# An attention and two-MoE kernel: value splitting and row scaling taken off GpSimd beside the attention, two fills and two weight splits put at its ends

## The chip, the cores and the metric

One core of a Trainium2 chip runs the whole program. The metric is the device time of one execution in microseconds (us), taken as the median of several executions. The engines are called TensorE (PE in the rows, PEld for its weight loads), VectorE (DVE), ScalarE (ACT), GpSimd (POOL) and SyncE (SP, which here only issues transfers).

## The reference

Three stages, each feeding the next, all in float32:

```python
scores = scale * q @ k.T                      # B, H, S, D = 2, 8, 768, 64
keep = is_sink | in_window                    # 4 sink columns, window 128
a = softmax(where(keep, scores, -1e9)) ; x = a @ v       # -> [1536, 512]
...
logits = x @ w_gate + modality_bias[modality_id]         # 8 experts
e_idx = argmax(logits) ; gate_w = probs[e_idx]
out[mask] = gate_w * (relu(x[mask] @ w1[e]) @ w2[e])     # routed MoE, F = 1024
...
P = exp(x @ w_gate2 - max) ; 8 x { rows /= sum ; columns /= sum ; P *= N/E }
out += P[:, e] * (relu(x @ w1[e]) @ w2[e])               # dense MoE, 8 experts
```

## The kernel before, in words

**Attention (`attention_fast`, L161-532).** There are 8 groups (batch b, pair of heads g) of 6 tiles of 128 query rows: 48 units. A unit is a chain over four engines. TensorE multiplies queries and keys (`sc`, L351), VectorE adds the mask and takes the row maximum (`pt`, `bias`, L353), ScalarE takes the exponential (L355), TensorE transposes (`tq`, L363), ScalarE and VectorE split the result into a high and a low 16-bit part (`ph` L381, `pl` L391), and TensorE multiplies both with the values (`po`, L409-L412). VectorE scales the result into `x_b` (L420-L425). Beside this, the four sink columns go through a small product: `psk` (L371 on ScalarE for its high part, L375 on VectorE for its low part), `tk` (L386) and L403. The loop (L477-529) handles a different phase of three neighbouring units in each turn.

**Values.** A group's values `raw_v` are prepared while the group ahead of it runs (`prep`, lists `e`, `m0`, ... at L329 ff. say in which turn). The scale is `vinv` (`r.inv`). For the first group ScalarE writes the high part with the scale (L327) and VectorE the low part (L328). For the other seven groups GpSimd multiplies `raw_v` in place (`v_sc`, L276, 128x768), ScalarE copies the high part (`v_hi`, L273, twice) and GpSimd subtracts (`v_lo`, L279, twice). GpSimd also makes the sink rows of the values (L289-L294).

**Routing of batch 0** runs as generator steps (`Steps`) inside the loop once its rows are there (from unit 18 on): logits, arg-max and positions on VectorE (`route`, L784-971). Then `scatters` (L749) multiplies each of 6 row tiles by its gate on GpSimd (L753) and writes its rows to their places in DRAM with an indirect transfer from GpSimd (L754). `weights0` (L772) loads the first expert's weights in quarters (q = 0, 1; tile `r`) and splits each into a high part on ScalarE (L780) and a low part (L781), for q = 0 on GpSimd and for q = 1 on VectorE. Its first split starts at turn `SPLIT0` = 43 ("late"), the others follow one turn at a time.

**Routed MoE (`routed`, L1290).** It multiplies the scattered rows (`xrow`, transposed at L986 and split into `xh`, `xl` at L991, L997) with the split weights (L1135, L1145); later weight quarters are split at L731. **Dense MoE** (L1509-1595) does the same for 8 experts with seven products in place of eight per block (`bk` L1518, `y` L1572).

**What sets the order.** The order on ScalarE and GpSimd in the attention is that of the program text (`manual_schedule`, L475); on VectorE and TensorE a scheduler orders the instructions after the first units. Each engine works through its own list in order. The start (`setup_consts`, L54) ends with `fi` (L105), which all engines load (L106) before they branch into `attention_fast` (L1086); behind the branch VectorE builds the masks (`masks_a`, L192) and GpSimd clears `xrow` (L662).

## Time and profile before

| | |
|---|---|
| median of 3 runs | 1295.49 us (1295.07 to 1298.07) |
| the profiled execution | 1297.28 us, span 1295.3 us |
| mean granted TensorE clock | 0.986 of full speed |
| busy share of the span: TensorE, VectorE, ScalarE, GpSimd | 97%, 74%, 45%, 34% |
| attention up to the first routed product | 0 to 149.33 us |
| dense MoE, TensorE alternating between L1518 and L1572 | about the last 870 us |

The span is the time from the first to the last instruction; the profiled execution adds what lies around it. A busy TensorE is not TensorE at its peak, since its matmuls overlap and their ends are modelled. The attention is 12% of the span, and its engines' loads differ from stage to stage, so the page's shares over the whole span say little of it; it has to be read by windows.

### The profile page before, as it was taken

Reading aid. Unit: us, or ns where it says so; the run is one execution under the profiler, and the core shown is the slowest. Engines: PE = TensorE matmul, PEld = TensorE weight load, DVE = VectorE, ACT = ScalarE, POOL = GpSimd, SP = SyncE. Lnnn points to the kernel's source line nnn. Section 1 sums busy time; section 2 is a strip of 40 time slices with the busy share of each in tenths; the row PEclk is TensorE's granted clock in tenths of the full one; section 3 lists DMA queues with packets and bytes.
Section 4 is the critical chain, followed back from the end, with each engine's and each line's share of the span. In section 5 each row is a group of like instructions: output and inputs, shape, how many; then the busy total and the mean of one; then the engine's idle time right before and its main releaser. Section 6 shows DMA issues by size and latency. Waiting matters only on the chain.

```text
span 1295.3 us, 19403 instructions
## 1 busy us (share of the span) xinstructions
PE 1250.8 (97%) x7201; PEld 748.4 (58%) x7201; DVE 958.5 (74%) x2096; ACT 582.2 (45%) x1087; POOL 446.1 (34%) x434
## 2 busy tenths in 40 slices
PE   6999799999899999999999999999999999999997
PEld 4666589998554555555555555555555555555553
DVE  7978585448599777777777777777777777777764
ACT  5876524556444364343433344343433344343431
POOL 2436230338503333333333334333333333333323
PEclk9998899999899999999999999999999999999999
DMA  6433626632101112121111112121111112221002
GB/s 132 109 68 122 186 82 198 195 110 72 50 5 37 37 39 54 40 53 38 37 37 38 37 37 49 46 54 37 37 38 37 37 38 46 48 53 38 5 1 97
DMA packets 114300, 80.16 MB, mean 62 GB/s; under 512 B 50196, under 2 KB 97300, under 8 KB 114196
## 3 DMA queue, kind: packets, MB, share of 16 engines
q1 hardware_dynamic: 112276, 72.51, 22.5%
q0 software_dynamic: 1920, 6.32, 1.3%
q8 instruction: 59, 0.97, 0.3%
q14 instruction: 45, 0.37, 0.1%
HBM read 71.94 MB, written 6.87 MB: 61 GB/s over the span
## 4 chain that ended last, share of the span: by engine, by line
PE 66%; DVE 3%; issue 3%; POOL 1%; ACT 1%; POOLq 0%; DVEq 0%
PE y L1572 35%; PE bk L1518 31%; DVE cb L1530 1%; DVE hl L1527 1%; POOL out_dram L1592 0%; DVE x L1585 0%; ACT hh L1524 0%; DVE xlo L1225 0%; ACT x L1583 0%; DVE wmax L1025 0%; DVE scr__6108 L1500 0%; POOL w2l L1082 0%; DVE pp L1501 0%; DVE pp L1493 0%; DVE xmm L1020 0%
## 5 line engine op out<-in xcount | busy, mean ns | idle before, releaser
L1585 DVE SCALAR_TENSOR_TENSOR x<-y,pps,x 128x512 f32<-128x512 f32 x332 | 243.8, 747 | 115.8 <-PE y L1572 115.7
L1572 PE MATMUL y<-w2h,hh 128*128 128x512 f16 x768 | 291.8, 380 | 1.0 <-DVE x L1585 0.5
L1572 PE MATMUL y<-w2l,hh 128*128 128x512 f16 x768 | 291.7, 380 | 0.0
L1572 PE MATMUL y<-w2h,hl 128*128 128x512 f16 x768 | 291.6, 380 | 0.0
L1530 DVE SCALAR_TENSOR_TENSOR cb<-bk,cb 128x384 f32<-128x384 f32 x384 | 189.8, 549 | 84.3 <-PE bk L1518 84.3
L1572 PEld LDWEIGHTS <-hh 128*128 128x128 f16 x1536 | 150.7, 98 | 174.9 <-issue 2.2
L1518 PEld LDWEIGHTS <-w1h 128*128 128x128 f16 x1792 | 175.4, 98 | 125.4 <-issue 4.6
L1059 POOL TENSOR_TENSOR xrow<-raw2a 128x256 f32<-128x256 f32 x160 | 112.6, 738 | 292.4 <-issue 245.0
L1524 ACT ACTIVATE hh<-cb 128x384 f16<-128x384 f32 x256 | 126.4, 523 | 174.5 <-DVE cb L1530 174.5
L1532 ACT ACTIVATE cb<-bk 128x384 f32<-128x384 f32 x64 | 31.3, 489 | 302.2 <-PE bk L1518 298.2
L1076 POOL TENSOR_TENSOR w1l<-raw2a,w1h 128x256 f16<-128x256 f32 x64 | 51.3, 821 | 300.3 <-ACT w1h L1064 300.3
L1518 PE MATMUL bk<-x_b,w1h 128*128 128x384 f16 x448 | 146.8, 328 | 1.7 <-DVEq L1423 1.7
L1518 PE MATMUL bk<-x_b,w1l 128*128 128x384 f16 x448 | 146.8, 328 | 0.0
L1518 PE MATMUL bk<-xl,w1h 128*128 128x384 f16 x448 | 146.8, 328 | 0.0
L1518 PE MATMUL bk<-xhi,w1l 128*128 128x384 f16 x448 | 146.0, 326 | 0.0
L1518 PE MATMUL bk<-xlo,w1h 128*128 128x384 f16 x448 | 146.0, 326 | 0.0
L1518 PE MATMUL bk<-xhi,w1h 128*128 128x384 f16 x448 | 146.0, 326 | 0.0
L1527 DVE SCALAR_TENSOR_TENSOR hl<-cb,hh 128x384 f16<-128x384 f32 x256 | 132.2, 557 | 8.0
L1572 PEld LDWEIGHTS <-hl 128*128 128x128 f16 x768 | 75.3, 98 | 91.1 <-issue 0.8
L1518 PEld LDWEIGHTS <-w1l 128*128 128x128 f16 x896 | 87.9, 98 | 58.4 <-issue 0.7
L1077 POOL TENSOR_TENSOR w1l<-xrow,w1h 128x1280 f16<-128x1280 f32 x32 | 84.7, 2647 | 0.1
L1082 POOL TENSOR_TENSOR w2l<-raw2b,w2h 128x1024 f16<-128x1024 f32 x32 | 68.7, 2148 | 12.6 <-ACT w2h L1081 12.6
(370 smaller groups left out, 1884.1 us busy)
## 6 DMA issues: line engine op xcount, KB each, us to landing
raw2b<-in_moe_w_dram SPq DMA_DIRECT2D x40, 512.0 KB, 3.8
raw2a<-in_moe_w_dram SPq DMA_DIRECT2D x64, 256.0 KB, 3.0
r<-in_moe_w_dram SPq DMA_DIRECT2D x24, 512.0 KB, 6.5
raw2a<-in_moe_w_dram SPq DMA_DIRECT2D x8, 512.0 KB, 5.0
wall<-dmax SPq DMA_DIRECT2D x32, 128.0 KB, 4.0
xrow<-scr SPq DMA_DIRECT2D x4, 832.0 KB
raw_v<-in_v_dram SPq DMA_DIRECT2D x8, 384.0 KB, 4.0
raw_k<-in_k_dram SPq DMA_DIRECT2D x14, 192.0 KB, 2.8
```

Source lines behind the costliest of these rows:

```text
L1059: nc.gpsimd.tensor_tensor(ws[:, s_], x, y, op)
L1076: nc.gpsimd.tensor_tensor(wl[:, 4 + i], w1_block(n, i, i), wh[:, 4 + i], ALU.subtract)
L1077: nc.gpsimd.tensor_tensor(wl[:, 0:5], ws, wh[:, 0:5], ALU.subtract)
L1082: nc.gpsimd.tensor_tensor(vl, raw2[n % 2][1], vh, ALU.subtract)
L1518: nc.tensor.matmul(bank, w[wi][:, WSLOT[m], k], X[xi][sb][m - 1][:, k], start=(first and i == 0), stop=(i == 5), skip_group_check=True)
L1524: nc.scalar.activation(h[0][:, i, l], cb[:, 2 * i + l], AF.Relu)
L1527: nc.vector.scalar_tensor_tensor(h[1][:, i, l], cb[:, 2 * i + l], 0.0, h[0][:, i, l], ALU.max, ALU.subtract)
L1530: nc.vector.scalar_tensor_tensor(x[0], bank, sign * HSC, x[1], ALU.mult, ALU.add)
L1532: nc.scalar.activation(c22, b0, AF.Copy, scale=HSC)
L1572: nc.tensor.matmul(y, h[hi_][:, i, l, t * P:(t + 1) * P], w[wi][:, i], start=(i == 0 and pi == 0), stop=(i == 1 and pi == 2))
L1585: nc.vector.scalar_tensor_tensor(dst, y, f if e == 0 else pps[n % 3][:, T:T + 1], acc, ALU.mult, ALU.add)
```

## The change

Five edits. **(1)** `v_sc` (L276) goes; for every group ScalarE writes the high part with the scale and VectorE makes the low part from `raw_v`, the scale and the high part in one instruction. **(2)** The first two mask instructions and the window's difference `wp` move from behind the branch to ahead of it. **(3)** `xrow` is cleared before the branch. **(4)** The row scaling of batch 0 (6 instructions) moves from GpSimd to ScalarE; that of batch 1, in the routed stage, stays. **(5)** The four splits of the first weights run at the ends of the loop's last four turns (46 to 49) in the order w1 of q 0, w1 of q 1, w2 of q 0, w2 of q 1, all low parts on GpSimd; each is followed by its own load of the next quarter.

```diff
-def setup_consts(nc, c, cp, a, first):
+def setup_consts(nc, c, cp, xp, a, first):
...
     nc.vector.tensor_copy(fi, fl[0:1, 3:4])
+    c.mk = xp.tile([P, 3, P + SB], F32, name="mk")
+    c.mtmp = xp.tile([P, P], F32, name="mtmp")
+    c.wp = xp.tile([P, 1], F32, name="wp")
+    keep_window(nc, c, c.mk[:, 2, SB:], c.dcur, c.mtmp)
+    nc.vector.tensor_single_scalar(c.wp, c.win, -float(P), ALU.add)
     c.fast = nc.values_load(fi[0:1, 0:1], engines=mybir.ALL_ENGINES, min_val=0, max_val=1)
...
     def masks_a():
-        nc.vector.tensor_single_scalar(tmp, c.dcur, 0.0, ALU.is_ge)
-        nc.vector.scalar_tensor_tensor(cur, c.dcur, c.win, tmp, ALU.is_lt, ALU.mult)
...
-        nc.vector.tensor_single_scalar(w1, c.win, -float(P), ALU.add)
-        nc.vector.tensor_scalar(prev, c.dcur, w1, None, ALU.is_lt)
+        nc.vector.tensor_scalar(prev, c.dcur, c.wp, None, ALU.is_lt)
...
         def v_hi(h):
-            nc.scalar.activation(r.vs[:, h, :, 0:DH], d["v"][:, h], AF.Copy)
-
-        def v_sc():
-            nc.gpsimd.tensor_tensor(rv, rv, r.inv.unsqueeze(2).broadcast_to([P, G * NT, DH]), ALU.mult)
+            nc.scalar.activation(r.vs[:, h, :, 0:DH], d["v"][:, h], AF.Copy, scale=r.inv)
 
         def v_lo(h):
-            nc.gpsimd.tensor_tensor(r.vs[:, h, :, V1:], d["v"][:, h], r.vs[:, h, :, 0:DH], ALU.subtract)
+            nc.vector.scalar_tensor_tensor(r.vs[:, h, :, V1:], d["v"][:, h], r.inv, r.vs[:, h, :, 0:DH], ALU.mult, ALU.subtract)
...
-        m0 = [[], [], [vs1], [], [vinv, v_sc], [], [], []]
+        m0 = [[], [], [vs1], [], [vinv], [], [], []]
...
-        if i == SPLIT0:
-            ready.append("late")
...
         steps.run("pool")
+        if i >= len(units) - 2:
+            steps.run("w")
...
-        setup_consts(nc, c, cp, a, first)
+        setup_consts(nc, c, cp, xp, a, first)
+    nc.gpsimd.memset(xrow, 0.0)
...
-        nc.gpsimd.memset(xrow, 0.0)
...
     def scatters(b, bank):
         xb = x_bs[b]
         for t in range(NT):
-            yield "pool", 2 if t else 0
-            nc.gpsimd.tensor_tensor(xb[:, t, 0:D], xb[:, t, 0:D], gs[:, t:t + 1].broadcast_to([P, D]), ALU.mult)
+            yield "pool" if b else "act", 2 if t else 0
+            if b:
+                nc.gpsimd.tensor_tensor(xb[:, t, 0:D], xb[:, t, 0:D], gs[:, t:t + 1].broadcast_to([P, D]), ALU.mult)
+            else:
+                nc.scalar.activation(xb[:, t, 0:D], xb[:, t, 0:D], AF.Copy, scale=gs[:, t:t + 1])
+                yield "pool", 0
...
-        for q in range(2):
-            for i in range(2):
-                yield ("act", 1) if q or i else ("late", 0)
+        for i in range(2):
+            for q in range(2):
+                yield "w", 0
                 h, l = wqs[q][2 * i:2 * i + 2]
                 nc.scalar.activation(h, raws[q][i], AF.Copy)
-                (nc.vector if q else nc.gpsimd).tensor_tensor(l, raws[q][i], f32(h), ALU.subtract)
-            load_raw(q, *wsrc(ex), 2 + q)
+                nc.gpsimd.tensor_tensor(l, raws[q][i], f32(h), ALU.subtract)
+                load_part(q, i, *wsrc(ex), 2 + q)
```

The lines of the changed kernel lie some 5 lower from L276 on, so that L353 is L348 there, L391 is L386, L375 is L370, and L780 and L781 are L785 and L786.

**VectorE around the branch.** First the list before, from `fi` on (`TENSOR_LOAD` and the comparison are the branch):

```order
L105 CAST fi<-fl 1x1
L106 TENSOR_LOAD fi
L1086 COMPARE_AND_BRANCH
L195 TENSOR_SCALAR mtmp<-dcur 128x128
L896 MEMSET tf 128x1
L196 SCALAR_TENSOR_TENSOR mk<-dcur,val,mtmp 128x128
L197 SCALAR_TENSOR_TENSOR mk<-jrow,val,mk 128x128
```

and the same place now:

```order
L104 CAST fi<-fl 1x1
L114 TENSOR_SCALAR mtmp<-dcur 128x128
L115 SCALAR_TENSOR_TENSOR mk<-dcur,val,mtmp 128x128
L109 TENSOR_SCALAR wp<-val 128x1
L110 TENSOR_LOAD fi
L1091 COMPARE_AND_BRANCH
L197 SCALAR_TENSOR_TENSOR mk<-jrow,val,mk 128x128
```

The window mask (`mtmp`, `mk`) and `wp` now stand between `fi` and VectorE's own load of it.

**VectorE in group 0, where the values of group 1 are split**, before (the two ISA rows of L353 are one masking step):

```order
L425 TENSOR_TENSOR x_b_76<-po,rc 128x2x128
L353 ISA pt,bias<-sc,mk 128x260
L353 ISA bias 128x1
L391 SCALAR_TENSOR_TENSOR pl<-tq,ph 128x512
L353 ISA pt,bias<-sc,mk 128x260
L353 ISA bias 128x1
L353 ISA pt,bias<-sc,mk 128x260
L353 ISA bias 128x1
L665 CAST mf<-mi 128x12
L420 TENSOR_SCALAR rc<-po,vinv 128x4
```

and now, where L274 is the low part of the values and L348 the masking step:

```order
L420 TENSOR_TENSOR x_b_76<-po,rc 128x2x128
L348 ISA pt,bias<-sc,mk 128x260
L348 ISA bias 128x1
L386 SCALAR_TENSOR_TENSOR pl<-tq,ph 128x512
L274 SCALAR_TENSOR_TENSOR vs<-raw_v,vinv,vs 128x6x64
L348 ISA pt,bias<-sc,mk 128x260
L348 ISA bias 128x1
L660 CAST mf<-mi 128x12
L348 ISA pt,bias<-sc,mk 128x260
L348 ISA bias 128x1
```

One low part now stands right behind a unit's `pl`, ahead of the next masking step; the second (not shown) stands behind the `pl` after it in the same way.

**ScalarE at the end of the attention**, before (`w1h`, `w2h` are the weights' high parts, L991 the high part of the routed rows):

```order
L780 ACTIVATE w2h_226<-r_1_219 128x1024
L371 ACTIVATE psk<-pt 128x16
L381 ACTIVATE ph<-tq 128x512
L388 ACTIVATE skT<-tk 24x128
L381 ACTIVATE ph<-tq 128x512
L388 ACTIVATE skT<-tk 24x128
L991 ACTIVATE xh<-tp 128x4x104 x4
```

and now:

```order
L376 ACTIVATE ph<-tq 128x512
L383 ACTIVATE skT<-tk 24x128
L785 ACTIVATE w1h_227<-r_0_223 128x1024
L376 ACTIVATE ph<-tq 128x512
L383 ACTIVATE skT<-tk 24x128
L785 ACTIVATE w1h_231<-r_1_225 128x1024
L785 ACTIVATE w2h_229<-r_0_224 128x1024
L996 ACTIVATE xh<-tp 128x4x104
L785 ACTIVATE w2h_233<-r_1_226 128x1024
L996 ACTIVATE xh<-tp 128x4x104 x3
```

Three of the four high parts now stand behind the last unit's `ph` (row L376), two of them ahead of the first L996 (L991 before) and one ahead of the other three. GpSimd's list ends with the four low parts in the same order and nothing between them, and on SyncE's list each is followed by the load that overwrites its raw quarter.

## Rows read from the trace of the kernel before

**Rows 1.** Windows behind the attention: us; busy (count) of PE, PEld, DVE, ACT, POOL; PEclk, DMA.

```profile
149.33:156.00 6.67, 6.67 (x26) 6.08 (x27) 0.00 (x0) 1.78 (x3) 0.00 (x0) 0.56 1.05 279
...
338.00:1295.30 957.30, 942.81 (x5029) 492.07 (x5029) 721.36 (x1401) 386.62 (x664) 312.05 (x285) 0.99 0.17 39
```

**Rows 2.** The same view, the attention: 17 units, then four times 6, then 5.

```profile
21.55:59.75 38.20, 37.85 (x388) 26.29 (x387) 35.86 (x149) 32.96 (x94) 14.06 (x26) 1.00 0.45 98
59.75:77.54 17.79, 17.32 (x160) 11.15 (x159) 12.05 (x50) 13.62 (x38) 5.51 (x11) 1.00 0.30 68
77.54:94.39 16.85, 16.45 (x178) 11.56 (x176) 14.74 (x68) 13.66 (x39) 5.26 (x10) 1.00 0.29 63
94.39:113.46 19.07, 17.31 (x133) 11.62 (x132) 17.75 (x75) 11.96 (x34) 11.51 (x16) 0.75 0.65 194
113.46:128.88 15.42, 14.35 (x144) 10.13 (x141) 13.33 (x52) 11.60 (x34) 11.07 (x16) 0.97 0.14 53
128.88:142.95 14.07, 9.59 (x85) 6.17 (x83) 12.71 (x32) 11.15 (x26) 6.79 (x9) 0.88 0.66 174
```

**Rows 3.** Line 375 alone: its durations, then its VectorE time (count) in those windows.

```profile
L375 DVE SCALAR_TENSOR_TENSOR psk<-pt,psk x32: 124/161/3405, 21.1 to 142.2; 128x8 f16<-128x8 f32 x32
...
21.55:59.75 38.20, 5.05 (x11) 1.00 0.45 98
94.39:113.46 19.07, 3.05 (x4) 0.75 0.65 194
113.46:128.88 15.42, 3.61 (x4) 0.97 0.14 53
128.88:142.95 14.07, 4.01 (x4) 0.88 0.66 174
```

**Rows 4.** Timeline behind the branch: start, duration, engine, line, instruction, [idle before <-releaser].

```profile
7.37 2.04 DVE L195 TENSOR_SCALAR mtmp<-dcur 128x128 f32<-128x128 f32 x1 [0.77 <-DVE fi L105]
7.44 1.81 POOL L662 MEMSET xrow<- 128x2048 f32 x1
```

**Rows 5.** Timeline at the first scatters.

```profile
98.85 1.17 POOL L754 DMA_INDIRECT scr<-x_b,pos  x1 [0.29 <-POOL x_b L753]
...
99.32 1.81 DVE L375 SCALAR_TENSOR_TENSOR psk<-pt,psk 128x8 f16<-128x8 f32 x1
...
100.05 1.05 POOL L753 TENSOR_TENSOR x_b<-x_b,rs 128x512 f32<-128x512 f32 x1
```

**Rows 6.** Timeline at the first weights' parts.

```profile
132.03 2.34 POOL L781 TENSOR_TENSOR w1l<-r,w1h 128x1024 fp32r<-128x1024 f32 x1
...
133.31 3.40 DVE L375 SCALAR_TENSOR_TENSOR psk<-pt,psk 128x8 f16<-128x8 f32 x1
...
136.77 0.23 PE L386 MATMUL tk<-ident_h,psk 128*24 128x128 f16 x1 [3.27 <-DVE psk L375]
```

**Rows 7.** Groups by line, up to 150 us: count | busy, mean ns | idle before.

```profile
L780 ACT ACTIVATE w1h<-r 128x1024 fp32r<-128x1024 f32 x2 | 2.1, 1040 | 0.0
L796 ACT ACTIVATE xT<-tp 128x512 f32<-128x512 f32 x6 | 3.5, 582 | 2.6 <-PE tp L792 2.6
L327 ACT ACTIVATE vs<-raw_v,vinv 128x384 f16<-128x384 f32 x2 | 1.1, 608 | 0.0
L328 DVE SCALAR_TENSOR_TENSOR vs<-raw_v,vinv,vs 128x384 f16<-128x384 f32 x2 | 1.1, 616 | 0.0
```

**Rows 8.** Line 279: idle of GpSimd before it and what ended it; us, times.

```profile
  ACT vs L273: 18.1, 13
```

**Rows 9.** Timeline from the attention's end into the routed stage.

```profile
145.55 0.55 PE L986 MATMUL tp<-ident,xrow 104*128 104x104 f32 x4 [0.48 <-DVE rc L422]
...
149.33 0.72 PE L1135 MATMUL pt<-xh,w1h 128*128 128x416 f32 x1 [3.23 <-issue]
...
160.08 1.05 ACT L731 ACTIVATE w1h<-r 128x1024 fp32r<-128x1024 f32 x1
```

**Rows 10.** Transfers: KB each, us from issue to landing.

```profile
r<-in_moe_w_dram SPq DMA_DIRECT2D x24, 512.0 KB, 6.5
```

More of the change, by code (lines that the diff above doesn't have):

```diff
@@ L41 @@
 LOAD_LAG = 6
-SPLIT0 = 43
 GW = P // KC
@@ L183, in attention_fast @@
     R = 3 * G * NS
-    mk = cp.tile([P, 3, P + SB], F32, name="mk")
-    tmp = cp.tile([P, P], F32, name="mtmp")
-    w1 = cp.tile([P, 1], F32, name="w1")
+    mk = c.mk
     hm = cp.tile([R, 3, G], F32, name="hm")
@@ L227, in prep @@
         bnk = {}
-        rv = d["v"].rearrange("p h t d -> p (h t) d")
         vd = r.vs.rearrange("p h t w -> p (h t) w")
@@ L326, in v_c @@
                 for h in range(G):
-                    nc.scalar.activation(r.vs[:, h, :, 0:DH], d["v"][:, h], AF.Copy, scale=r.inv)
-                    nc.vector.scalar_tensor_tensor(r.vs[:, h, :, V1:], d["v"][:, h], r.inv, r.vs[:, h, :, 0:DH], ALU.mult, ALU.subtract)
+                    v_hi(h)
+                    v_lo(h)
             r.v_s = v_sink
@@ L721, in body, with load_part @@
     wqs = [new_wq(wr, i) for i in range(2)]
+    def load_part(i, j, w1, w2, q):
+        if j:
+            nc.sync.dma_start(raws[i][1], w2.rearrange("o (k p) f -> p (o k) f", p=P)[:, q * FC:(q + 1) * FC, :])
+        else:
+            nc.sync.dma_start(raws[i][0], w1.rearrange("o (k p) f -> p (o k) f", p=P)[:, :, q * FQ:(q + 1) * FQ])
     def load_raw(i, w1, w2, q):
-        nc.sync.dma_start(raws[i][0], w1.rearrange("o (k p) f -> p (o k) f", p=P)[:, :, q * FQ:(q + 1) * FQ])
-        nc.sync.dma_start(raws[i][1], w2.rearrange("o (k p) f -> p (o k) f", p=P)[:, q * FC:(q + 1) * FC, :])
+        for j in range(2):
+            load_part(i, j, w1, w2, q)
     def split_w(ri, wi, pool_lo=False):
@@ L751, in scatters @@
         for t in range(NT):
-            yield "pool", 2 if t else 0
-            nc.gpsimd.tensor_tensor(xb[:, t, 0:D], xb[:, t, 0:D], gs[:, t:t + 1].broadcast_to([P, D]), ALU.mult)
+            yield "pool" if b else "act", 2 if t else 0
+            if b:
+                nc.gpsimd.tensor_tensor(xb[:, t, 0:D], xb[:, t, 0:D], gs[:, t:t + 1].broadcast_to([P, D]), ALU.mult)
+            else:
+                nc.scalar.activation(xb[:, t, 0:D], xb[:, t, 0:D], AF.Copy, scale=gs[:, t:t + 1])
+                yield "pool", 0
             o = nc.gpsimd.indirect_dma_start(
```

## Prediction, made before the change ran

> **What bounds the kernel now.** I read the stages behind the attention first, to learn whether time saved early reaches the end. In the last 957 us TensorE is busy for 942.81 us [rows 1]: it is the bound there and takes its weights as it goes, so a routed stage that begins earlier ends earlier by the same amount, unless a load is late. That leaves the attention, which I read by windows between units, because its load changes from stage to stage [rows 2]. The reader should see three things there. In the first window 17 units take 38.20 us, 2.25 us each, with VectorE busy for 35.86 us and ScalarE for 32.96 us; TensorE shows 37.85 us busy, which counts its latencies too. With TensorE and VectorE both near full, a us less on one of them need not be a us less for the stage. The next two windows carry the routing; VectorE has room in them. In the last three GpSimd's load doubles, from about 5 us to 11.51 and 11.07 us, and the pace drops to as much as 3.2 us a unit.
>
> Why it drops is seen in one small VectorE instruction, line 375. Its median is 0.161 us and its longest 3.405 us [rows 3]. The long ones lie beside long GpSimd work: one starts at 99.32 us, in the middle of an indirect transfer, and ends at 101.13 us, as does the row scaling (100.05 + 1.05 = 101.10 us) that follows it [rows 5]; another starts at 133.31 us during the first of GpSimd's two weight splits, each 2.34 us, and lasts 3.40 us, over the rest of that one and the whole of the next, while TensorE sits idle for 3.27 us waiting for it [rows 6]. The first mask instruction takes 2.04 us beside a fill of 1.81 us [rows 4]. So VectorE stands still while GpSimd works, and the stall spans several GpSimd instructions if they follow without a gap. The change takes this GpSimd work away or moves it to where VectorE has nothing of that kind.
>
> Stalled time on line 375, from [rows 3], is its busy time less 0.161 us for each: 3.28 us in the first window (11 instructions), 2.41, 2.97 and 3.37 us in the last three, 12.0 us in all. With the 1.8 us of the mask I count 13.8 us; some routing instructions are also stretched, which I take inside the stage terms.
>
> **The change part by part.** All terms are against the profiled execution (span 1295.3 us, 1297.28 us in all), which is 1.8 us above the median of 1295.49 us; I apply the sum to the median.
>
> *Start.* The fill moves to where VectorE waits for its first inputs, and two mask instructions ahead of the branch, where they add some 0.6 us of VectorE's own time before it branches, in place of 2.04 + 0.35 us behind. The mask instruction without the fill is 2.04 - 1.81 = 0.23 us. The gain is at most 1.8 us. The next thing late is TensorE's first score product and its slow clock at the start, so I bound it from 0.8 to 1.8 us and take **-1.5**, nearer the row's own figure.
>
> *Values in the first window (three groups prepared).* Stalls of 3.28 us go; six low parts come to VectorE at 0.616 us each (line 328 in [rows 7]), 3.7 us. GpSimd's time saved is worth nothing in itself. The scale rides on ScalarE's high part; that does the same work at 0.608 us (line 327 in [rows 7]), covered by ScalarE's idle 38.20 - 32.96 us; without that cover it would cost at most a tenth of a us each. Bounds: -3.3 (low parts hidden) to +0.4. I take **-0.6**, as the window has hardly a gap for anything new on VectorE.
>
> *Second and third window.* VectorE has 17.79 - 12.05 us idle in the second, so two low parts mostly hide: **+0.3** (0 to +1.1). In the third, routing instructions were stretched and two low parts come: **-0.4** (-1.5 to +0.6).
>
> *Fourth window.* The stall of 2.41 us, and what the scatters add to the routing's instructions, go. Its low clock (0.75) starts after such a stall, and I expect it to go with it. But ScalarE gets three row scalings at about 0.582 us (the nearest row is a 128x512 copy, line 796 [rows 7]): 11.96 + 1.75 = 13.7 us busy. The two windows where it was that full took 17.79 and 16.85 us, the one after took 15.42 us with the same amount of units. So 15.0 to 17.8 us are the ends; I take 15.6, close to the shorter end because the routing's products on TensorE, which lengthened the second and third window, are not here: **-3.5** (-4.1 to -1.3).
>
> *Fifth window.* 2.97 us of stalls go, three row scalings and two low parts come: 13.3 us busy on ScalarE, 11.6 us on VectorE. **-0.9** (-3.0 to +0.5), since ScalarE takes most of it back.
>
> *Last five units.* 14.07 us for five units that prepare no further group. At the first window's 2.25 us they would be 11.3 us; one weight part on ScalarE (line 780, 1.04 us [rows 7]) stands ahead of the last `ph` and costs about half of that. Stalls, the 3.27 us gap and the other weight work between the units are gone: **-3.3** (-4.0 to -2.0).
>
> *Tail.* Here the change pays. Three of ScalarE's 1.04 us weight parts now stand behind the last unit, two ahead of the first high part of the routed rows and one ahead of the rest. These rows go through TensorE, ScalarE and VectorE by way of two banks, so the last transposition, which began at 145.55 us [rows 9], comes some 2.5 us later after the last `pl`. From its end, 146.10 us, TensorE stood 3.23 us without a wait that the profile shows, until 149.33 us [rows 9]; I leave that gap as it is. The routed stage's first 6.67 us then ran at a granted clock of 0.56 [rows 1], the lower of the two levels for most of it; TensorE stands idle no less ahead of it now, so I expect the same there. **+2.4** (+0.8 to +3.1, all three parts).
>
> GpSimd's four splits follow one another, 4 x 2.34 = 9.4 us, and SyncE's loads for the next quarters stand behind them. They begin about a us before the last `pl`, so the load behind the third is issued some 6.4 us after that `pl` and, at 6.5 us to landing [rows 10], is there after 13 us. Its first reader, line 731, came 10.7 us after the first routed product [rows 9], which I put some 9 us after the last `pl`: needed at about 20 us. So I cost it at nothing; the cover is 6 to 7 us. No VectorE instruction of the kind of line 375 is left behind these splits.
>
> Sum: -1.5 - 0.6 + 0.3 - 0.4 - 3.5 - 0.9 - 3.3 + 2.4 = -7.5 us, so 1295.49 - 7.5 = **1288.0 us** (1289.8 us for a profiled execution).
>
> **A rule against a row.** Six indirect transfers stay on GpSimd beside the attention. The row shows line 375 held from the middle of one [rows 5]; if each still holds VectorE for the 0.7 us between 99.32 us and the transfer's end at 100.02 us, six cost up to 4 us. I take 0.5 us within the fourth and fifth terms, as few will meet such an instruction. The Trainium skill (SBUF — State Buffer, "Who interferes with whom") says that a VectorE instruction with two SBUF inputs contends only with a GpSimd instruction that reads SBUF, and infers that writing descriptors does not stop one; by that the cost would be nothing and the sum 0.5 us lower. The row speaks against it, though it can't part the transfer from the scaling behind it.
>
> **The rivals.**
> 1. *The freed time is taken back.* TensorE and VectorE are near full in the first window, ScalarE becomes full in the fourth and fifth. Then only the start, half of the fourth term, and the last two remain: -1.5 - 1.8 - 3.3 + 2.4 = -4.2, **1291.3 us**. For it: the busy times of [rows 2]. Against: line 375 feeds TensorE late in the chain. Chance 0.18. The Trainium skill (Perfetto Trace Analysis, "Optimizing Scalar/DVE Operations") warns in the same sense that shifting work between GpSimd and VectorE might not help since they share a port.
> 2. *All of it comes through.* VectorE's stalls bound every stage, and the new work fits into idle time: -13.8 - 3.3 (the clock and the routing's part of the fourth window and the weights in the last) + 2.4 = -14.7, **1280.8 us**. Against: VectorE has 2.3 us idle in 38.20. Chance 0.15.
> 3. *VectorE waits in line (slower).* A low part waits for ScalarE's high part, and behind it in VectorE's list stands the masking step that feeds the whole unit. GpSimd waited 18.1 us for these high parts in 13 cases, 1.4 us each [rows 8]; GpSimd kept nobody waiting by that, VectorE would. If all 14 wait so, 14 x 1.4 = 19.5 us less the gain: **1307.5 us**; eight of them decide it, as 8 x 1.4 = 11.2 us is the gain and the 3.9 us above it. Against: in the order, each low part stands behind a `pl` whose `ph` stands behind that high part. Chance 0.07.
> 4. *The stalls only move.* The low parts read two SBUF operands like line 375, and GpSimd's sink rows and transfers remain: line 375 and now line 274 could be held by them. The stall terms of the first, fourth and fifth window shrink to a fifth (-1.0), the start stays (-1.5), the last units and the tail give -0.9: -3.4 plus some 1.5 us of new stalls, **1293.6 us**. Against: what remains is 0.3 us pieces, no 1.5 us ones. Chance 0.08.
>
> **How the numbers follow.** The forecast has 0.52. A measurement of this kernel can tell about 0.3% or 3.9 us from no change, so "faster" begins under 1291.6 us. It holds the forecast, rival 2 and under half of rival 1: 0.74. "Same" has the rest of rival 1 and rival 4 and a little of the forecast's upper end: 0.18; "slower" has rival 3 and mishaps in the tail: 0.08. The range takes the forecast's own bounds (1284 to 1291.5), rival 2 nearly and rivals 1 and 4: 1280.5 to 1293.7 us.
>
> **What would show it.** Line 375 (L370 after) with a maximum under 1 us; the low parts (L274) at 0.6 us, 14 of them more than before; no GpSimd row longer than 1.2 us ahead of the last units; no window at a clock of 0.75 before the routed stage; the first masking step about 1.5 us earlier; the first routed product near 142 us in place of 149.33 us, with the same 3.2 us gap ahead of it, and line 731 without a wait on a load. The prediction is wrong if the fifth window keeps its 15.4 us and the fourth its 19 us (rival 1), if L274 shows 1 us or more (rivals 3 and 4), or if the gap ahead of the routed stage grows past 6 us.

## The result and the profile after

| | before | after |
|---|---|---|
| median of 5 runs each | 1295.07 us (1293.32 to 1298.07) | 1280.18 us (1279.44 to 1280.76) |
| ratio of the times | | 0.9894 [0.9881, 0.9908] |
| profiled execution, its span | 1297.28, 1295.3 us | 1280.76, 1278.9 us |
| first routed product | 149.33 us | 134.66 us |
| start of the last dense product on `y` | 1286.25 us | 1271.86 us |

The change gains 14.9 us, 1.1%. The forecast was 1288.0 us, 7.5 us faster; the measured median lies 0.3 us under the low end of its range (as a difference, 14.9 us where the range goes to 15.0), and within 1 us of rival 2 (1280.8 us). The routed stage begins 14.67 us earlier and the last product of the dense stage 14.4 us earlier: what the attention gained was handed on almost whole, as the forecast's first step said. The two profiled executions differ by 2 us more than that; this lies behind the last product, a stretch that no edit touches.

The windows of the attention after the change, the same units as in [rows 2] (columns as there):

```profile
19.48:55.41 35.93, 35.93 (x387) 25.14 (x387) 34.34 (x155) 33.74 (x94) 4.88 (x17) 1.00 0.50 111
55.41:71.26 15.85, 15.83 (x160) 10.68 (x157) 13.07 (x53) 13.54 (x38) 1.95 (x7) 1.00 0.35 79
71.26:89.63 18.37, 18.37 (x182) 12.90 (x181) 14.50 (x71) 14.41 (x39) 1.97 (x7) 1.00 0.26 58
89.63:104.21 14.58, 13.78 (x137) 9.45 (x136) 13.92 (x75) 13.66 (x38) 5.25 (x10) 1.00 0.71 206
104.21:117.05 12.84, 12.70 (x137) 8.63 (x135) 12.26 (x54) 12.78 (x36) 5.33 (x10) 1.00 0.31 116
117.05:125.43 8.38, 8.08 (x94) 5.46 (x93) 7.38 (x30) 8.08 (x23) 2.31 (x7) 1.00 0.47 104
125.43:134.66 9.23, 2.37 (x29) 1.68 (x27) 3.82 (x8) 4.80 (x8) 8.86 (x4) 0.78 0.52 160
```

Look first at the granted clock: the fourth window and the two after it stood at 0.75, 0.97 and 0.88 in [rows 2], and no window is under 1.00 now before the tail, the last row. Then at VectorE and ScalarE: in the fifth window ScalarE is busy for 12.78 of 12.84 us, TensorE for 12.70 and VectorE for 12.26, so all three are nearly full, yet these units take 2.6 us less than before.

By stage, in us against the profile of before:

| stage | forecast | measured |
|---|---|---|
| start | -1.5 | -2.07 |
| first window (17 units) | -0.6 | -2.27 |
| second and third | +0.3, -0.4 | -1.94, +1.52 |
| fourth | -3.5 | -4.49 |
| fifth | -0.9 | -2.58 |
| last five units | -3.3 | -5.69 |
| tail, to the first routed product | +2.4 | +2.85 |
| sum | -7.5 | -14.67 |

The second and third window came out with the other sign than forecast, nearly cancelling each other; of the rest every term has its sign, and every gain came out larger. Line 370, the one that stood still as line 375 in [rows 3], the values' low part, the new row scaling, and the copy at L292 that experiments below return to; their durations in the changed kernel (min/median/max in ns, first and last start, shape):

```profile
L370 DVE SCALAR_TENSOR_TENSOR psk<-pt,psk x32: 134/154/333, 19.1 to 123.4; 128x8 f16<-128x8 f32 x32
L274 DVE SCALAR_TENSOR_TENSOR vs<-raw_v,vinv,vs x16: 608/612/619, 16.1 to 116.4; 128x384 f16<-128x384 f32 x16
L757 ACT ACTIVATE x_b<-x_b,rs x6: 703/706/711, 92.9 to 113.7; 128x512 f32<-128x512 f32 x6
L292 DVE COPY kb<-kb x8: 158/158/170, 9.1 to 107.7; 128x24 f32<-128x24 f32 x8
```

The longest L370 went from 3.405 to 0.333 us and the stalls of 12.0 us are gone. No low part stretches, all 16 take 0.61 us, and VectorE stood idle ahead of them for 0.2 us in all.

The tail and the routed stage's start, as a timeline (start, duration, engine, line, instruction, [idle before it <- what ended it]):

```profile
125.46 1.04 ACT L785 ACTIVATE w1h<-r 128x1024 fp32r<-128x1024 f32 x1
126.41 1.04 ACT L785 ACTIVATE w2h<-r 128x1024 fp32r<-128x1024 f32 x1
127.36 0.49 ACT L996 ACTIVATE xh<-tp 128x416 fp32r<-128x416 f32 x1
127.75 1.04 ACT L785 ACTIVATE w2h<-r 128x1024 fp32r<-128x1024 f32 x1
...
129.96 0.55 PE L991 MATMUL tp<-ident,xrow 104*128 104x104 f32 x4 [0.80 <-DVE xl L1002]
...
134.66 0.71 PE L1140 MATMUL pt<-xh,w1h 128*128 128x416 f32 x1 [4.15 <-issue]
```

Two weight parts stand ahead of the first `xh` and one behind it, as foreseen, and the last transposition starts 4.5 us after the last `pl` (125.43 us) where it took 2.6 us [rows 2, 9]. Behind it TensorE stood 4.15 us with no wait that the profile shows, in place of 3.23.

### The profile page after: what moved, and what is told of

It is laid out like the page before. It is cut to its first block, busy times and chain, and to the rows that moved or that the text cites. A ratio compares the mean times of both kernels' runs of the same rounds, so it can differ in the third digit from the quotient of the medians.

```text
span 1278.9 us, 19395 instructions
## 1 busy us (share of the span) xinstructions
PE 1242.8 (97%) x7201; PEld 744.1 (58%) x7201; DVE 946.4 (74%) x2108; ACT 586.4 (46%) x1093; POOL 422.5 (33%) x409
## 4 chain that ended last, share of the span: by engine, by line
PE 67%; DVE 3%; issue 3%; POOL 1%; ACT 1%; POOLq 0%; DVEq 0%
PE y L1577 35%; PE bk L1523 31%; DVE cb L1535 1%; DVE hl L1532 1%; POOL out_dram L1597 0%; DVE x L1590 0%; ACT hh L1529 0%; DVE xlo L1230 0%; ACT x L1588 0%; DVE wmax L1030 0%; DVE scr__6100 L1505 0%; POOL w2l L1087 0%; DVE pp L1506 0%; DVE pp L1498 0%; DVE xmm L1025 0%
```

## The experiments

The kernels that undo or add one thing were timed beside the kernel before, and each ratio is to that kernel. Differences to the change are between medians of different series, in which the median of the kernel before itself lay between 1293.18 and 1295.66 us; a difference of 1 or 2 us is therefore near the noise. The stage times are of one profiled execution each.

**u1_start: the start put back.** The two mask instructions and `wp` go back behind the branch, the clearing of `xrow` to where it was.

```diff
-    keep_window(nc, c, c.mk[:, 2, SB:], c.dcur, c.mtmp)
-    nc.vector.tensor_single_scalar(c.wp, c.win, -float(P), ALU.add)
...
-    nc.gpsimd.memset(xrow, 0.0)
...
+        keep_window(nc, c, cur, c.dcur, c.mtmp)
...
+        nc.gpsimd.memset(xrow, 0.0)
```

> The changed kernel with its start as before: the window mask and wp behind the branch, xrow cleared there. If the start's gain of 2.1 us (first pl at 13.44 for 15.52 us) goes through to the end, this is 2.1 us slower than the change, 12.8 us faster than the kernel before, and the first pl stands near 15.5 us again with the mask instruction near 2.0 us. If the later stages swallow it (loads or the slow clock at the start set the pace), under 0.7 us slower.

1281.81 us, 0.991 [0.9883, 0.9936]: 1.6 us over the change (2.1 expected), the routed stage 2.37 us later. The first mask instruction is held beside the fill again:

```profile
7.39 2.03 DVE L112 TENSOR_SCALAR mtmp<-dcur 128x128 f32<-128x128 f32 x1 [0.77 <-DVE fi L104]
7.45 1.81 POOL L657 MEMSET xrow<- 128x2048 f32 x1
```

In the changed kernel that instruction takes 0.20 us. The start is worth about its whole stall.

**u2_values: the values' scale and low parts on GpSimd again.**

```diff
-            nc.scalar.activation(r.vs[:, h, :, 0:DH], d["v"][:, h], AF.Copy, scale=r.inv)
+            nc.scalar.activation(r.vs[:, h, :, 0:DH], d["v"][:, h], AF.Copy)
...
+            nc.gpsimd.tensor_tensor(rv, rv, r.inv.unsqueeze(2).broadcast_to([P, G * NT, DH]), ALU.mult)
...
-            nc.vector.scalar_tensor_tensor(r.vs[:, h, :, V1:], d["v"][:, h], r.inv, r.vs[:, h, :, 0:DH], ALU.mult, ALU.subtract)
+            nc.gpsimd.tensor_tensor(r.vs[:, h, :, V1:], d["v"][:, h], r.vs[:, h, :, 0:DH], ALU.subtract)
```

> The changed kernel with the values' scaling (128x768) and low parts back on GpSimd for seven groups. Held-up theory (VectorE stands still beside GpSimd): line 370 shows stalls near 1.2 us again, one to a group, some 7 us of them; VectorE loses 14 low parts at 0.61 us = 8.6 us, so by VectorE's time alone this would be about even; since a stall comes late in a unit and a low part does not, I expect 1 to 4 us slower than the change. Rival (VectorE's load is the bound): 1.5 us faster than the change.

1289.01 us (1285.12 to 1291.47, 8 runs), 0.9965 [0.9946, 0.9985]: 8.8 us over the change by the medians, 6.2 us by the routed stage's start in the profile, more than the 1 to 4 us expected. The stalls on the line of L370 are back only in the first window, 3.4 us in place of the 7 us expected. That window is what it was before the change, with six low parts fewer on VectorE than the change has:

```profile
19.52:57.72 38.20, 37.85 (x388) 26.30 (x387) 35.86 (x149) 32.96 (x94) 14.06 (x26) 1.00 0.47 103
57.72:75.52 17.80, 17.32 (x160) 11.15 (x159) 12.06 (x51) 13.64 (x38) 5.52 (x11) 1.00 0.30 69
```

So 8.6 us of VectorE work less (14 low parts at 0.612) and GpSimd's work back made the kernel slower. Not all of that need be holds: VectorE's order changes with its list, and the second window, in which that line has no stall, takes 17.80 us for 15.85. d1 and o1 below part the two.

**u3_scatter: the row scaling of batch 0 back on GpSimd.**

```diff
-            yield "pool" if b else "act", 2 if t else 0
-            if b:
+            yield "pool", 2 if t else 0
+            if True:
```

> The changed kernel with the six row scalings of batch 0 back on GpSimd. Held-up theory: line 370 shows stalls of 0.9 to 1.8 us beside them and a routing instruction or two near 1.5 us; 3 to 6 us slower than the change. My prediction's view (ScalarE takes most of it back, at 0.71 us each): 0 to 1.5 us slower.

1286.7 us, 0.9944 [0.9924, 0.9964]: 6.5 us over the change, a little more than expected. A timeline of it, with the pattern of [rows 5]:

```profile
97.09 1.96 DVE L905 TENSOR_SCALAR rk<-beg,tf 128x8 f32<-128x8 f32 x1
97.96 1.05 POOL L755 TENSOR_TENSOR x_b<-x_b,rs 128x512 f32<-128x512 f32 x1
...
99.28 1.01 POOL L759 DMA_INDIRECT scr<-x_b,pos  x1 [0.28 <-POOL x_b L755]
...
99.64 1.80 DVE L370 SCALAR_TENSOR_TENSOR psk<-pt,psk 128x8 f16<-128x8 f32 x1
...
100.37 1.04 POOL L755 TENSOR_TENSOR x_b<-x_b,rs 128x512 f32<-128x512 f32 x1
```

and its third and fourth window, where the change takes 18.37 and 14.58 us at a clock of 1.00:

```profile
71.28:92.45 21.17, 21.17 (x182) 14.80 (x181) 14.62 (x71) 14.53 (x39) 1.98 (x7) 0.84 0.22 50
92.45:114.13 21.68, 18.66 (x142) 12.28 (x140) 18.42 (x75) 13.15 (x37) 8.31 (x13) 0.76 0.55 171
```

The third window ends before the first scaling on GpSimd (95.44 us) and has no stall on L370, and TensorE was busy throughout; yet the granted clock fell in it, which cost this execution 2.8 us. So a slower clock does not need a hold, and of the 9.5 us by which the routed stage begins later here than in the change (144.16 for 134.66 us), these 2.8 are not the scalings' own.

L905 takes 0.22 us in the changed kernel (at 93.15 us). In that kernel the six transfers remain but no scaling follows them on GpSimd:

```profile
93.85 1.17 POOL L759 DMA_INDIRECT scr<-x_b,pos  x1 [1.19 <-ACT psk L366]
...
94.61 0.16 DVE L910 TENSOR_TENSOR m<-m,jrow 128x16 f32<-128x16 f32 x1
...
107.31 1.01 POOL L759 DMA_INDIRECT scr<-x_b,pos  x1 [0.19 <-ACT pt L350]
...
107.59 0.15 DVE L370 SCALAR_TENSOR_TENSOR psk<-pt,psk 128x8 f16<-128x8 f32 x1
```

Instructions with two inputs that start late in a transfer (94.61) or early in one (107.59) are not held. So what held line 375 in [rows 5] was the scaling behind the transfer.

**u4_weights: the first weights' splits in their old turns**, q by q, from turn 43 on, with the low parts of q 1 on VectorE.

```diff
+        if i == 43:
+            ready.append("late")
...
-                yield "w", 0
+                yield ("act", 1) if q or i else ("late", 0)
...
-                nc.gpsimd.tensor_tensor(l, raws[q][i], f32(h), ALU.subtract)
-                load_part(q, i, *wsrc(ex), 2 + q)
+                (nc.vector if q else nc.gpsimd).tensor_tensor(l, raws[q][i], f32(h), ALU.subtract)
+            load_raw(q, *wsrc(ex), 2 + q)
```

> The changed kernel with the first weights' splits as before: from turn 43 on, one a turn, two low parts on GpSimd and two on VectorE. Held-up theory: one stall of 2.3 to 3.4 us on line 370, TensorE idle behind it, a slow clock after it; the last five units take 13 to 14 us in place of 8.4, the tail gives back 2.9 us: 2 to 4 us slower than the change. Rival (the tail's loss eats the gain): within 1 us of it.

1285.17 us, 0.9939 [0.9918, 0.996]: 5.0 us over the change, where 2 to 4 had been expected. GpSimd's two splits, from its part of the timeline:

```profile
120.75 2.34 POOL L788 TENSOR_TENSOR w1l<-r,w1h 128x1024 fp32r<-128x1024 f32 x1
123.07 2.34 POOL L788 TENSOR_TENSOR w2l<-r,w2h 128x1024 fp32r<-128x1024 f32 x1
```

VectorE's part has the hold over the rest of the first split and the whole of the second:

```profile
122.32 3.11 DVE L370 SCALAR_TENSOR_TENSOR psk<-pt,psk 128x8 f16<-128x8 f32 x1
```

and its last five units:

```profile
117.63:131.92 14.29, 10.80 (x82) 6.62 (x82) 12.13 (x32) 11.02 (x26) 6.48 (x8) 0.76 0.67 171
```

They take 5.9 us more than in the change, of which the hold explains some 3; the tail is 2.1 us shorter (7.15), since less of the work is left for it.

The four parts undone singly cost 1.6 + 8.8 + 6.5 + 5.0 = 21.9 us, more than the 14.9 us that they give together. A part's price therefore depends on what else is there. In u3 and u4 TensorE's granted clock falls to 0.76 over the stage that holds the stall, which is a cost beside the stall's own length; whether that makes the sum too large was not separated.

**d1_read and d2_write: is it GpSimd's reading that holds VectorE?** Both are the changed kernel with unused GpSimd work on scratch memory of its own, three pieces per group where `v_sc` and `v_lo` stood; one multiplies, the other only fills. VectorE has the same instructions in the same order as in the change, but both kernels also clear the scratch at the start, and the first three pieces follow there; this delays the first `pl` by 2.9 us in d1 and by 1.5 us in d2.

```diff
+        def dummy(n):
+            x = dum[:, 0:n].rearrange("p (a b) -> p a b", b=DH)
+            nc.gpsimd.tensor_tensor(x, x, x, ALU.mult)
...
+        m0 = [[], [], [vs1], [], [vinv, L(dummy, 768)], [], [], []]
```

and in d2 the pieces of 768, 384 and 384 columns are fills of 1660, 1000 and 1000:

```diff
+        def dummy(n):
+            nc.gpsimd.memset(dum[:, 0:n], 0.0)
```

> The changed kernel with GpSimd work put back that nobody waits for: for each of seven groups one product of a scratch tile with itself (128x768) and two of 128x384, at the turns where the scaling and the low parts stood. It computes nothing that is used. Held-up theory (VectorE stands still while GpSimd reads and writes SBUF): stalls on line 370 and now on the low parts (line 274, two SBUF operands) of up to 1.5 us; 3 to 8 us slower than the change. Rival (what counted was GpSimd's place in the chain, its results being waited for): within 0.7 us of the change.

> As the run with reading scratch work, but fills of about the same lengths (128x1660 and 128x1000) in place of products: GpSimd only writes. If any GpSimd work holds VectorE, as the first mask instruction beside the fill of xrow suggests: as slow as the reading run, 3 to 8 us. If a fill holds only copies, casts and products with a constant, but no instruction with two SBUF operands: line 370 and 274 keep 0.15 and 0.61 us, and the time is within 1 us of the change.

d1: 1289.98 us, 0.9969 [0.9956, 0.9981], 9.8 us over the change. d2: 1283.23 us, 0.9909 [0.9885, 0.9934], 3.05 us over it. In d1 the product `psk` reaches 1.906 us again (0.333 in the change, 0.330 in d2), and a low part is held as well:

```profile
110.80 1.95 POOL L274 TENSOR_TENSOR dum<-dum 128x384 f32<-128x384 f32 x2
...
110.99 1.07 DVE L280 SCALAR_TENSOR_TENSOR vs<-raw_v,vinv,vs 128x384 f16<-128x384 f32 x1
```

In d2 they are not (the same line takes 0.15 us in the middle of a fill), but a copy is:

```profile
47.92 2.47 POOL L273 MEMSET dum<- 128x1660 f32 x2
...
48.30 0.15 DVE L375 SCALAR_TENSOR_TENSOR psk<-pt,psk 128x8 f16<-128x8 f32 x1
48.38 1.06 DVE L297 COPY kb<-kb 128x24 f32<-128x24 f32 x1
48.46 0.98 DVE L256 TENSOR_SCALAR vmm<-vmm 1x1 f32<-1x1 f32 x1
48.52 1.24 DVE L353 CUSTOM_DVE_ANT_0 pt<-sc,mk 128x260 f32<-128x260 f32 x1
```

The first row joins two fills; the first of them, 128x1660, takes 1.52 us and ends at 49.44 us. There the copy L297 ends too (48.38 + 1.06). The operation and the masking step behind it end late with it; whether a fill would hold them by themselves these rows do not show.

So unused GpSimd work, which waits for nothing VectorE makes and for which nothing waits, costs about what the real work cost (9.8 - 2.9 = 6.9 us, against 6.2 to 8.8 in u2); the hold is of the engines against each other, not a wait in the program. Nor is it the time that the pieces take in GpSimd's own list: d2's fills are as long (23.7 us in all, the products 22.4) and stand at the same places, and cost 3.05 - 1.5, some 1.5 us. The hold depends on both instructions. A GpSimd product holds both kinds (L899 of the kernel before, with one input, took 1.03 us beside a row scaling, and 0.15 us as L904 of the change); a fill holds the copies and not the products with two inputs in SBUF. The copy at L292 of the change (0.158 us) had a maximum of 1.708 us in d2. The Trainium skill (SBUF — State Buffer, "Who interferes with whom") says the same of VectorE operations with two inputs in SBUF, that only a GpSimd instruction that reads SBUF stops them; these two traces agree with it.

**n1_noscale and n2_nolo: what does the added work cost?** n1 leaves out the row scaling of batch 0 (the gates), n2 puts zero fills, on VectorE too, in place of all 16 low parts (the values' low halves are missing).

```diff
-                nc.scalar.activation(xb[:, t, 0:D], xb[:, t, 0:D], AF.Copy, scale=gs[:, t:t + 1])
...
-            nc.vector.scalar_tensor_tensor(r.vs[:, h, :, V1:], d["v"][:, h], r.inv, r.vs[:, h, :, 0:DH], ALU.mult, ALU.subtract)
+            nc.vector.memset(r.vs[:, h, :, V1:], 0.0)
```

> The changed kernel without the six row scalings of batch 0 on ScalarE (6 x 0.71 us); the gates of that batch are left out of the computation. My prediction's view that ScalarE is the bound in these two stages: 2 to 4 us faster than the change. If TensorE and VectorE cover it: within 0.7 us.

> The changed kernel with the 14 low parts of the values on VectorE (0.61 us each, 8.6 us) replaced by fills of zeros; the low parts are left out of the computation. Prediction's view (VectorE near full, a low part costs the stage about what it takes): 5 to 8 us faster than the change. Rival (TensorE and the chain through the unit set the pace, VectorE has room): 0 to 2.5 us faster.

n1: 1277.97 us, 0.9868 [0.9844, 0.9892], 2.2 us under the change, of which 1.33 us before the routed stage; the difference is no larger than the interval, and by the median it just reaches the 2 to 4 us expected of a ScalarE that is the bound, by the profile it does not. Its fifth window took 11.94 us for 12.84, the fourth 14.40 for 14.58, together 1.1 us for 6 x 0.706 = 4.24 us of ScalarE. So in these windows some three quarters of ScalarE's added work stood in time that was free. VectorE's order in n1 is that of u3 through the whole attention, so these two also price the scalings on GpSimd: u3 is 8.7 us slower than n1.

n2: 1278.58 us, 0.9887 [0.9869, 0.9904], 1.6 us under the change, 1.18 us at the routed stage's start. It does not price the low parts. The fills stay on VectorE and take 0.378 us each for 0.612, so 3.3 us of the 14 low parts' 8.6 us went, not all of it. A fill also waits for no values, so VectorE's order changed, and the first window became longer than the change's 35.93 us with six low parts fewer (first row: count | busy, mean ns | idle before):

```profile
L274 DVE MEMSET vs<- 128x384 f16 x16 | 6.0, 378 | 0.5
19.43:55.93 36.50, 36.43 (x388) 25.42 (x389) 33.76 (x153) 33.86 (x94) 3.99 (x14) 1.00 0.50 111
```

The expectation of 5 to 8 us was thus not put to a test here; what the low parts cost is better read from o1.

**o1_short: the kernel before, with GpSimd's work made short.** VectorE's list is the old one, row for row. The scaling runs over 8 of 768 columns, and fills take the place of the low parts; most of the scaling and the values' low halves are thus left out.

```diff
-            nc.gpsimd.tensor_tensor(rv, rv, r.inv.unsqueeze(2).broadcast_to([P, G * NT, DH]), ALU.mult)
+            nc.gpsimd.tensor_tensor(rv[:, 0:1, 0:8], rv[:, 0:1, 0:8], r.inv.unsqueeze(2).broadcast_to([P, 1, 8]), ALU.mult)
...
-            nc.gpsimd.tensor_tensor(r.vs[:, h, :, V1:], d["v"][:, h], r.vs[:, h, :, 0:DH], ALU.subtract)
+            nc.gpsimd.memset(r.vs[:, h, :, V1:], 0.0)
```

> The kernel before, its instruction order on VectorE the same row for row, with the values' work on GpSimd cut short: the scaling covers 8 columns in place of 768, the low parts are filled with zeros. What the values' low parts and most of their scaling give is left out. If GpSimd's hold on VectorE alone cost the first three windows their time: line 375 has no stall near 1.2 us before 60 us, and the first window takes about 36 us for 38.2; the second and third window, which had hardly a stall on line 375, keep 17.8 and 16.9 us. If VectorE's order as well made the difference in the second window (15.9 us in the changed kernel), it shows here by the 17.8 us that stay. In all 3 to 6 us faster than the kernel before. If neither the hold nor the order counts there (the values' results being waited for did): the second window falls to 16 us too.

1290.1 us, 0.9975 [0.9966, 0.9985]: 3.1 us faster than the kernel before; the routed stage 6.1 us earlier in its profile.

```profile
21.47:57.17 35.70, 35.49 (x386) 25.01 (x385) 32.33 (x150) 33.10 (x94) 7.48 (x26) 1.00 0.46 98
57.17:74.87 17.70, 17.47 (x162) 11.38 (x161) 12.04 (x52) 13.53 (x38) 2.87 (x10) 1.00 0.34 73
...
109.61:122.26 12.65, 12.56 (x138) 8.83 (x137) 11.18 (x52) 11.58 (x34) 9.12 (x16) 1.00 0.18 68
```

The first window falls from 38.20 to 35.70 us by the holds alone; the change, which has six low parts more on VectorE there, takes 35.93. So the holds on line 375, 3.4 us there (5.05 us [rows 3] less 1.62 us on L370 now), were worth some 2.5 us, and the change's low parts, 3.7 us of VectorE, took back about 0.2, if the two orders on VectorE are otherwise worth the same. The fills that remain on GpSimd here hold hardly anything (no L297 over 0.383 us). The second window stays at 17.70 where the change has 15.85. With the third (16.42 here) the sum is 34.12 us, against 34.64 before and 34.22 in the change: the new order on VectorE moved about 1.8 us from the second window to the third, and hardly any was gained. Over the first three windows the change, with ten low parts (6.1 us) more, takes 70.15 us for 69.82 here. The fifth window, 15.42 us before, takes 12.65 here with the row scalings still on GpSimd, and 12.84 in the change with three of them on ScalarE and two low parts more.

**t1_tail and t2_tail: can the tail be had for less?** In t1 only the first weight split stands before the routed rows' high parts and the other three behind them; in t2 the first split too moves behind the last unit's `ph`, to between the second and third `xh`.

```diff
-        if i >= len(units) - 2:
+        if i == len(units) - 2:
             steps.run("w")
-    steps.drain()
+    for th in list(steps.threads):
+        while th in steps.threads:
+            steps.step(th)
```

```diff
+    ths = list(steps.threads)
+    for _ in range(3):
+        steps.step(ths[0])
+    steps.step(ths[-1])
+    for th in ths:
+        while th in steps.threads:
+            steps.step(th)
```

> The changed kernel with only the first weight split ahead of the routed rows' high parts; the other three follow them. If ScalarE's three 1.04 us copies cost the tail what the trace shows (last transposition 5.1 us behind the last pl for 3.2 us before, first routed product 9.2 us behind it for 6.4 us): 2 to 3 us faster than the change, the first routed product 6.5 to 7.2 us behind the last pl, and no wait for the later loads. If the gap ahead of the routed stage is set by something else (instructions of the next part being fetched): 0 to 1 us faster.

> The run with the other three weight splits behind the routed rows' high parts, and the first one too moved from ahead of the last ph to between the second and third of these high parts, where ScalarE stood 0.55 us idle. If the copy ahead of the last ph held the last unit up: 0.3 to 0.8 us faster than that run (1277.9 us), and 2.5 to 3 us faster than the change. If its low part on GpSimd (2.34 us) is then late for the third routed product: the same as that run or up to 1 us slower.

t1: 1277.91 us, 0.987 [0.9846, 0.9895]; its tail takes 6.69 us in place of 9.23 and the routed stage begins at 132.64 us, 2.0 us earlier:

```profile
132.64 0.68 PE L1142 MATMUL pt<-xh,w1h 128*128 128x416 f32 x1 [3.86 <-ACT w2h L787]
```

In this kernel the profile no longer calls that gap one without a wait: it ends with the last of ScalarE's copies (`w2h`). So the copies put behind the `xh` may still hold the product up; this was not separated.

t2: 1280.44 us, 0.9899 [0.9881, 0.9918]; its routed stage began at 132.41 us and it was no faster than t1, where 0.3 to 0.8 us had been expected.

> The run with three weight splits behind the routed rows' high parts once more, with more rounds, to tell it from the change (ratio 0.9894, 0.9881 to 0.9908). If its routed stage begins 2 us earlier in every execution: ratio 0.987 to 0.988 with an interval that ends under 0.9894. If the first figure was luck of the clock: 0.989 or more.

The same kernel as t1, once more: 1280.46 us (1279.15 to 1282.7), 0.9885 [0.9862, 0.9908]. The routed stage began at 132.29 us and the last dense product started at 1268.72 us, 3.1 us earlier than in the change, but the program's end came only 0.6 us earlier (span 1278.3 for 1278.9), as the stretch behind that product was longer. So the ends of the chain agree that t1 shortens the tail, and the time does not: by its intervals t1 can't be told from the change. No version that surely beats it was found.

## Why the prediction fell short

*The direction and the mechanism stood.* VectorE was held by GpSimd's work, the holds ended with it (12.0 us of stalls on line 375 to none), no window had a clock of 0.75 any more, and the tail paid some of it back. Undoing each part brings stalls back (u1 to u4), and unused work brings back the same (d1). That the holds alone cost the clock is not shown: in u3 it also fell in a window without one. The size was half, and the terms that failed are these:

- **"As the window has hardly a gap for anything new on VectorE"** (first window, -0.6; measured -2.27). This is the step that failed most plainly. Of the low parts' 3.7 us it charged 2.7, against 3.3 us of stalls. VectorE busy for 35.86 of 38.20 us [rows 2] looked full, but that busy time held the stalls themselves. By o1 the low parts cost about 0.2 us there, and ten of them about 0.3 us in the first three windows. Why they cost so little, with VectorE still busy for 34.34 of 35.93 us, was not shown; they stand behind a `pl`, where the next masking step may not have been due. The bound of -3.3 "low parts hidden" was the nearer one.
- **"Since ScalarE takes most of it back"** (fifth window, -0.9; measured -2.58). ScalarE is full in this window (12.78 of 12.84 us), but n1 prices three scalings there at 0.9 us and all six at 1.1 us, though each is longer than was taken (0.706, not 0.582 us), and o1 without them is only 0.2 us shorter there. For the fourth window, two windows of before in which ScalarE was that full were read as what a full ScalarE costs; the change's fourth takes 14.58 us with as much ScalarE work, so something else made those long. That it was the routing on VectorE and TensorE is likely, but was not tested.
- **Fourth window** (-3.5; measured -4.49, beyond its bound of -4.1): right in kind, short for the same reason. u3 shows what a single remaining source of holds does there: 21.68 us, at a clock of 0.76.
- **Last five units** (-3.3; measured -5.69): they were priced at the first window's 2.25 us a unit, 11.3 us. They take 1.68, for they prepare no further group; the rows of before gave no unstalled unit of that kind to read it from, and only the fact that no group is prepared was there to be used.
- **Second and third** (+0.3 and -0.4; measured -1.94 and +1.52): their sum was forecast well (-0.1; measured -0.42) and each alone was wrong; o1 shows it as order on VectorE.
- **Start** (-1.5; measured -2.07): u1 confirms the mechanism. It was taken a little too small; in the profile all of the stall and 0.2 us more came through.
- **Tail** (+2.4; measured +2.85): right in size and bounds, in part by luck. The last transposition comes 1.9 us later behind the last `pl`, where 2.5 had been forecast, and TensorE's wait behind it, which had been left as it was, grew by 0.9 us, from 3.23 to 4.15. Line 732 (L731 before) had no wait on a load, at 145.53 us, as forecast.

*The rivals.* The time is that of rival 2, and its condition held in the main: most of the new work stood in idle time, as far as o1 (6.1 of the 8.6 us on VectorE) and n1 (4.24 us on ScalarE) show. But not wholly, and some of the stalls may have been worth less than their length (2.5 of 3.4 us in o1), while others were worth more (u3, u4); its sum of -14.7 comes out by errors of both signs. Rival 1's condition, ScalarE full in the fifth window, held without its consequence. Rival 3 did not occur: VectorE stood idle for 0.2 us ahead of all L274, and none took over 0.62 us. Rival 4 fell with the maximum of 0.333 us on L370.

*The rule against the row.* The row was misread. Line 375 in [rows 5] was held by the scaling behind the indirect transfer and not by the transfer: where only the transfer remains, L370 and L910 take 0.15 and 0.16 us. That the hold began some 0.7 us before the scaling showed as running follows from this, but no row shows why. The trace of before already had rows that part the two, a transfer with no scaling right behind it:

```profile
101.38 1.01 POOL L754 DMA_INDIRECT scr<-x_b,pos  x1 [0.28 <-POOL x_b L753]
...
101.62 0.16 DVE L905 TENSOR_TENSOR m<-m,jrow 128x16 f32<-128x16 f32 x1
```

The Trainium skill (SBUF — State Buffer, "Who interferes with whom") was right in what it infers, that writing descriptors stops no such instruction, and here [rows 5], read alone, misled; the 0.5 us taken for the transfers should have been nothing. The rule of the Trainium skill that speaks against such a change (Perfetto Trace Analysis, "Optimizing Scalar/DVE Operations") is not borne out by this kernel: moving the values' work from GpSimd to VectorE and ScalarE gained 6 to 9 us, as u2, which takes that back, shows.

*What stays open.* Why the four parts undone singly add up to 21.9 us, of which the clock that u3's profile lost without a hold can be a part; why the added low parts cost so little; why TensorE stands 3.2 to 4.2 us ahead of the first routed product; and what lengthens the end of the program behind the last product by up to 2.6 us from one execution to another.

## What to carry to other kernels

Read the longest execution of a tiny instruction on one engine beside what the others run at that time: where it ends with another engine's instruction, suspect that the one holds the other, and that the busy time includes the waiting. Before charging work that moves to such an engine in full, subtract these stalls from its busy time and ask which instructions have slack behind them; here six low parts of 0.61 us cost the first window about 0.2 us. When work is taken out to learn its price, look whether something is left in its place on the same engine, and whether the order stays; n2's fills stayed on VectorE and changed its order. And give each part of a change its own undoing, since the parts' prices need not add up.

## What the runs showed of the hardware

A fill on GpSimd doesn't hold a VectorE product with two inputs in SBUF (0.15 us, d2) but does hold a copy of 24 columns (1.06 us for 0.158, d2) and a mask instruction with one input (2.03 us for 0.20, u1) beside it, so a fill is harmless or costly by what stands next to it. One held instruction stood through parts of two GpSimd splits in a row, 3.11 us (u4) and 3.40 us [rows 6], longer than the 2.34 us of either. And where such a hold let TensorE stand for 2.56 us or more, its granted clock over the last five units was 0.76 (u4) and 0.88 [rows 2, 6], while it was 1.00 there in the change, without the hold. A hold isn't needed for that: in u3 the clock was 0.84 over a window in which TensorE was busy for all of its 21.17 us.
